# Attention and a four-expert layer on one core: the order of one product's terms, where weight splits stand, and which engine empties one bank

## The chip, the cores and the metric

The kernel runs on one core of a Trainium2 chip. The metric is the time of one execution on the device, in microseconds; the lower, the better. The kernel before was run three times: 935.79, 936.87 and 939.62 us, median 936.87 us.

## What is computed

Attention over 4 x 8 heads (sequence 576, head size 64, causal, with a decay that a running sum gives), then a layer of four experts over the 2304 tokens of 512 numbers that come out of it. All inputs and outputs are fp32. Cut to the expert layer, which is what the change touches:

```python
p = domain_probs / (domain_probs.sum(-1, keepdims=True) + 1e-09)
out = np.zeros((N, D), dtype=np.float32)           # N = 2304, D = 512
for e in range(E):                                 # E = 4
    h = np.maximum(x @ w1[e], 0.0)                 # w1[e]: 512 x 1024
    out += p[:, e:e + 1] * (h @ w2[e])             # w2[e]: 1024 x 512
```

## The kernel before

The program has two stretches. Up to about 386 us the attention runs, interleaved with expert 0, which is computed plainly; its order comes from a planner. From there on only experts 1 to 3 run, and their order is the order in which the code is written: each engine has its queue, and takes its instructions in that order.

Numbers are fp32, but PE multiplies a rounded form of them. So each operand is kept as a high part (a copy by ACT, `hi`, L457) and a low part (the operand less its high part, by DVE or POOL, `sub`, L444). A product is the sum of three terms: high by high, high by low, low by high.

An expert's 1024 hidden numbers are taken as two halves, so there are six halves for experts 1 to 3 (`HALVES`). For each half the tokens pass in three groups of 768 (`g` 0, 1, 2), which makes 18 items. An item has a first layer (x by w1) and a second layer (h by w2). Each is a 2 x 2 block product done with seven products instead of eight, numbered 1 to 7, at the price of sums of blocks made ahead. One product is 12 matmuls (128 x 128 by 384 columns): two output banks, and for each two slices of the sum and the three terms. `product` (L1262) writes them. The list of terms has the weights' low part third; with `late`, which only the first product of a second layer of group 0 uses (L1395), both banks get the first two terms first, and the low-weight terms follow for both.

The layers alternate: the first layer of item w + 1 stands ahead of the second layer of item w (loop at L1432). Banks: bA is pb0 and pb1, bB is pb2 and pb3, bC is pb4 and pb5, bM the two banks of mo.

- `first_layer` (L1284) runs products 1, 6, 5, 7, 2, 4, 3. Between them partial sums are passed on: by ACT from bank to bank (`pass_on`, L1273) or from a bank to SBUF (`keep`, L1297, L1300), by DVE with an addition (`plus`, L1305, L1307) and a gate (`gate` or `relu_op`, L1278), which is the relu and the token's probability. The results are four blocks, c11, c12, h21 and c22. From the second item on h21 is gated in its banks; for the first item DVE gates it from bA into SBUF.
- The blocks and their sums (s5, s6, s7, s3, DVE L1055) become the second layer's operands: high part by ACT, low part by DVE or POOL (hT, xg and hx). The tables `START`, `EARLY`, `REST` say after which product each is issued.
- `second_layer` (L1377) runs products 1, 6, 2, 5, 7, 3, 4. Product 1 goes to bC; ACT passes it on to bB, and product 6 is added to it in bC. DVE adds results to the accumulators (`update`, L1385).

The weights of a half are loaded whole, then `w_steps` (L1125) makes eight steps of them: the sums (POOL, L1055), and for each of the seven products a split of the weight block into high part (ACT) and low part. Parts 4 and 6 need sums that POOL makes after other parts are split. The steps wait in the list `side`; after each product one of them, none or two are issued (`after`, L1288 and L1389). For the second-layer weights of halves 1 to 5 the sums stand in the second layer of group 2 of the half before, and all seven splits in the first layer that follows it, in the order 5, 1, 6, 2, 7, 3, 4, with all low parts on DVE. For half 0 all stand in the first item's first layer.

Of the kernel before, what the change touches and what calls it, by code (L numbers as in the profile page):

```python
# [326 lines left out]
def body(ctx, tc, qk, qkv0, vp, s, dp, w1, w1s, w2, w2s, out):  # L327
# [21 lines left out]
    late = {}  # L349
# [775 lines left out]
    def w_steps(which, begin=False):  # L1125
# [19 lines left out]
        def split(o, e):  # L1145
            hi("ACT", part(o, 0), src[o])
            sub(e, part(o, 1), src[o], part(o, 0).bitcast(F32))
            if begin:
                pass
            elif o == 5 and neg:  # L1150
                add("POOL", src[6], src[5], b[1, 1], ALU.subtract)
            elif o == 5:
                add("POOL", src[6], b[1, 1], src[5], ALU.subtract)
            if o == 2 and not begin:
                add("POOL", src[4], src[4], src[6], ALU.add if neg else ALU.subtract)
# [4 lines left out]
            ((5, "DVE"), (1, "DVE"), (6, "DVE"), (2, "DVE"), (7, "DVE"), (3, "DVE"), (4, "DVE")))]  # L1160
# [101 lines left out]
    def product(o, x, ts, start, part=w1_part, late=False):  # L1262
        wv = [part(o, l).rearrange("p (k f) -> p k f", k=2) for l in range(2)]
        terms = list(enumerate(((0, 0), (0, 1), (1, 0))))
        for u, some in [(0, terms[:2]), (1, terms[:2]), (0, terms[2:]), (1, terms[2:])] if late else [(0, terms), (1, terms)]:
            for k, (n, (wl, xl_)) in [(k, x) for x in some for k in range(2)] if late else [(k, x) for k in range(2) for x in some]:
                nc.tensor.matmul(ts[u], wv[wl][:, k, 128 * u:128 * u + 128], x[xl_][:, k, :],  # L1267
                                 start=start and k == 0 and n == 0, stop=k == 1 and n == 2, skip_group_check=not start)

    def product2(o, ts, start, late=False):  # L1270
        product(o, [h_part(o, l) for l in range(2)], ts, start, w2_part, late)
# [12 lines left out]
    def first_layer(w_i, at, tmp):  # L1284
# [3 lines left out]
        def after(o):  # L1288
# [4 lines left out]
            for _ in range((0, 2)[o == 3] if side and w_i and o in (4, 3) else 1 if w_i else 2):  # L1293
                if side:
                    side.pop(0)()
# [41 lines left out]
        tmp["h21"] = bA if w_i else [(t := temp())[:, 0], t[:, 1]]  # L1337
        for u in range(2):
            relu_op("DVE", tmp["h21"][u], bA[u], gp[:, 1], ALU.mult)
# [37 lines left out]
    def second_layer(w_i, n, g, at):  # L1377
# [17 lines left out]
        product2(1, bC, True, g == 0)  # L1395
# [36 lines left out]
    for w_i, (n, g) in enumerate(work):  # L1432
# [20 lines left out]
        if g == 2 and more:  # L1453
            w2_next = w_steps(2)
            side.append(w2_next.pop(0))
# [35 lines left out]
```

## Time and profile before

| | before |
|---|---|
| time, median of 3 runs | 936.87 us (935.79 to 939.62) |
| the profiled execution: time, span | 936.36 us, 934.6 us |
| PE busy | 915.2 us, 98% |
| PE weight loads busy | 884.4 us, 95% |
| DVE busy | 691.4 us, 74% |
| ACT busy | 479.4 us, 51% |
| POOL busy | 486.2 us, 52% |
| chain that ended last | PE 81%, DVE 8%, ACT 4%, POOL 3%, issue 3% |

A profile is one execution. Its busy time counts, for each engine, the time in which an instruction ran; matmuls are pipelined, so a busy PE may still run below its pace. In the view of waits an engine's idle time is put down to the instruction that released it, the one that came last. In a timeline each row is one or several equal instructions in a queue, with the idle time ahead of the first and its releaser in brackets. DVE's "t<-pb" means that it reads a PSUM bank and writes to SBUF; "pb<-hT_r,w2h" is a matmul of the second layer with the high weights, "pb<-x,w1h" one of the first. Instructions that follow each other on DVE overlap by some hundredths of a microsecond in the rows.

### The profile page before, as it was taken

The page shows a single profiled execution, that of the slowest core. Times are in us where ns is not written, and L with a number is a line of the kernel's source. Part 1 is how long each engine was busy: PE and PEld are TensorE (multiplying, and loading weights), DVE is VectorE, ACT ScalarE, POOL GpSimd, SP SyncE. Part 2 cuts the span into 40 slices and gives each one's busy share as a digit, 9 for nine tenths or more (in the row PEclk, how much of TensorE's full clock was granted, in tenths as well). Part 3 has the DMA queues.
Part 4 walks back from the last instruction along what each step waited for, and adds up shares of the span by engine and source line. Part 5 has one row for each costly group of instructions (what it writes and reads, how often), then busy time and mean ns, then how long its engine had stood idle before and what let it go on. Part 6 is the DMA issues. An engine that isn't in the chain of part 4 may idle for free.

```text
span 934.6 us, 16455 instructions
## 1 busy us (share of the span) xinstructions
PE 915.2 (98%) x5590; PEld 884.4 (95%) x5590; DVE 691.4 (74%) x1575; ACT 479.4 (51%) x1092; POOL 486.2 (52%) x524
## 2 busy tenths in 40 slices
PE   9999999999999999999999999999999999999998
PEld 6789999899999999989998999899989998999898
DVE  7878888887851122597978787978796879687985
ACT  6898999998860111434335352535244433444342
POOL 4688887887734697211644363446144713571222
PEclk9999999999999999999999999999999999999999
DMA  6788888878516974596587547855686467755603
GB/s 169 185 253 245 221 232 227 236 209 250 165 55 222 372 266 162 168 341 235 185 298 236 177 172 266 268 188 170 226 297 211 158 220 263 251 161 169 236 30 118
DMA packets 131039, 198.85 MB, mean 213 GB/s; under 512 B 11448, under 2 KB 107772, under 8 KB 130956
## 3 DMA queue, kind: packets, MB, share of 16 engines
q1 hardware_dynamic: 130956, 197.81, 66.4%
q8 instruction: 44, 0.72, 0.3%
q14 instruction: 39, 0.32, 0.1%
HBM read 154.85 MB, written 29.05 MB: 197 GB/s over the span
## 4 chain that ended last, share of the span: by engine, by line
PE 81%; DVE 8%; ACT 4%; POOL 3%; issue 3%; DMA 0%; ACTq 0%; POOLq 0%; DVEq 0%
PE pb L1267 40%; PE mo L1267 8%; PE mo L950 7%; PE mo L936 6%; PE pv L835 4%; PE pb L936 4%; PE pb L950 3%; PE T L785 3%; PE S L739 2%; DVE t L1278 2%; PE S L736 1%; DVE t L1307 1%; ACT a L758 1%; PE X L785 1%; DVE w2l L444 1%
## 5 line engine op out<-in xcount | busy, mean ns | idle before, releaser
L1267 PE MATMUL pb<-x,w1h 128*128 128x384 f32 x1008 | 257.8, 336 | 1.9 <-DVE t L1278 1.9
L1267 PEld LDWEIGHTS pb<-x,w1h 128*128 128x128 f32 x1008 | 182.2, 189 | 3.8 <-DVE t L1278 2.2
L1267 PE MATMUL pb<-x,w1l 128*128 128x384 f32 x504 | 169.1, 335 | 0.0
L444 POOL TENSOR_TENSOR hT_r<-t,hT_r 128x768 fp32r<-128x768 f32 x17 | 32.1, 1888 | 254.1 <-PE pb L1267 218.9
L1275 ACT ACTIVATE pb<-pb 128x384 f32<-128x384 f32 x106 | 49.8, 475 | 157.4 <-DVE t L1307 90.6
L457 ACT ACTIVATE hT_r<-t 128x768 fp32r<-128x768 f32 x72 | 60.8, 845 | 104.0 <-PE pb L1267 97.4
L1267 PE MATMUL pb<-hT_r,w2h 128*128 128x384 f32 x432 | 107.4, 336 | 1.4 <-DVE t L1278 1.4
L1267 PEld LDWEIGHTS pb<-x,w1l 128*128 128x128 f32 x504 | 95.2, 189 | 0.0
L758 ACT ACTIVATE a<-a,mx 128x576 f32<-128x576 f32 (+4 forms) x136 | 81.0, 597 | 12.9 <-DVE mx L750 9.3
L1385 DVE TENSOR_TENSOR acc<-pb,acc 128x384 f32<-128x384 f32 x144 | 74.8, 551 | 15.8 <-PE pb L1267 12.9
L1267 PE MATMUL pb<-xg,w2h 128*128 128x384 f32 x288 | 74.0, 337 | 8.6 <-ACT pb L1275 8.6
L1267 PEld LDWEIGHTS pb<-hT_r,w2h 128*128 128x128 f32 x432 | 77.4, 188 | 3.3 <-DVE t L1278 3.3
L936 PE MATMUL mo<-xg,w1h 128*128 128x384 f32 (+1 forms) x304 | 78.3, 327 | 0.0
L452 POOL TENSOR_SCALAR a<-a,sm 128x576 f32<-128x576 f32 (+5 forms) x111 | 60.6, 552 | 28.4 <-DVE sm L766 15.0
L444 DVE TENSOR_TENSOR hT_r<-t,hT_r 128x768 fp32r<-128x768 f32 x55 | 57.6, 1049 | 21.1 <-ACT hT_r L457 19.9
L1267 PE MATMUL pb<-hT_r,w2l 128*128 128x384 f32 x216 | 69.3, 334 | 0.0
L1307 DVE TENSOR_TENSOR t<-pb,t 128x384 f32<-128x384 f32 x74 | 37.6, 549 | 34.6 <-ACT t L1300 23.4
L1267 PEld LDWEIGHTS pb<-xg,w2h 128*128 128x128 f32 x288 | 51.5, 188 | 10.9 <-ACT pb L1275 10.9
L1055 DVE TENSOR_TENSOR t<-t 128x768 f32<-128x768 f32 (+1 forms) x40 | 59.5, 1494 | 0.0
L950 PE MATMUL mo<-hT_r,w2h 128*128 128x256 f32 (+1 forms) x320 | 58.3, 314 | 0.0
L814 DVE TENSOR_TENSOR aTl<-T,aTh 128x256 fp32r<-128x256 f32 (+2 forms) x103 | 51.3, 508 | 4.9 <-ACT aTh L457 3.7
L750 DVE CUSTOM_DVE_ANT_0 a<-S,mask 128x448 f32<-128x448 f32 (+4 forms) x107 | 48.1, 456 | 7.5 <-PE S L736 5.8
(216 smaller groups left out, 2312.4 us busy)
## 6 DMA issues: line engine op xcount, KB each, us to landing
x<-xs_d SPq DMA_DIRECT2D x68, 768.0 KB
x<-x_d SPq DMA_DIRECT2D x55, 768.0 KB
xs_d<-x SPq DMA_DIRECT2D x12, 768.0 KB
KK<-AB_r SPq DMA_DIRECT2D x24, 288.0 KB
osb<-p_d SPq DMA_DIRECT2D x18, 384.0 KB
xg<-x_d SPq DMA_DIRECT2D x16, 384.0 KB
w1r<-in_w1s_dram SPq DMA_DIRECT2D x6, 1024.0 KB
w2r<-in_w2s_dram SPq DMA_DIRECT2D x6, 1024.0 KB
```

Of the source, the lines that this page charges most:

```text
L444: (nc.gpsimd if e == "POOL" else nc.vector).tensor_tensor(out=out, in0=in0, in1=in1, op=ALU.subtract)
L452: (nc.gpsimd if e == "POOL" else nc.vector).tensor_scalar(out, in_, scale, 1.0 if bias is None else bias, op0=ALU.mult, op1=ALU.mult if bi ...
L457: nc.scalar.activation(out, in_, AF.Copy)
L750: nc.vector.tensor_tensor_reduce(out=z[0:n, j0:j1], in0=tok["S", (c, pi)][0:n, 0:j1 - j0], in1=mask[0:n, 448 - a + j0:448 - a + j1], scale ...
L758: nc.scalar.activation(z[0:n, 0:bb], z[0:n, 0:bb], AF.Exp, bias=tok["mx", c][0:n, k:k + 1], scale=-1.0, accum_out=tok["sm", c][0:n])
L814: nc.vector.tensor_tensor(out=dst, in0=src, in1=h_.bitcast(F32), op=ALU.subtract)
L936: nc.tensor.matmul(t[:, 0:w], wl[q][:, dc, o:o + P], xgt[:, l, dc, 0:w], start=(u == 0), stop=(u == 3 * KD - 1))
L950: nc.tensor.matmul(t[:, 0:w], wl[fc // 2][:, fc % 2, 128 * dt:128 * dt + 128], ht[:, fc, 0:w], start=(u == 0), stop=(u == 3 * KF - 1))
L1055: (nc.gpsimd if e == "POOL" else nc.vector).tensor_tensor(out=out, in0=in0, in1=in1, op=op)
L1267: nc.tensor.matmul(ts[u], wv[wl][:, k, 128 * u:128 * u + 128], x[xl_][:, k, :], start=start and k == 0 and n == 0, stop=k == 1 and n == 2, ...
L1275: nc.scalar.activation(out[u], in_[u], AF.Copy)
L1385: nc.vector.tensor_tensor(out=d, in0=ts[u], in1=d, op=ALU.add)
```

## The change

Four things are changed. The first product of a second layer of group 0 uses the usual order of terms; `late` is gone. The second-layer weights are split in the order 1, 2, 5, 6, 7, 3, 4, with part 7's low part on POOL; the sum for part 4 is issued after part 6 instead of part 2. For halves 1 to 5 the sums and the splits 1, 2 and 5 stand in the second layer of group 2, and the splits 6, 7, 3 and 4 in the first layer behind it. For the first item h21 is copied out of bA by ACT and gated in SBUF by DVE.

```diff
--- before.py
+++ after.py
@@ -1151,13 +1151,13 @@
                 add("POOL", src[6], src[5], b[1, 1], ALU.subtract)
             elif o == 5:
                 add("POOL", src[6], b[1, 1], src[5], ALU.subtract)
-            if o == 2 and not begin:
+            if o == (6 if neg else 2) and not begin:
                 add("POOL", src[4], src[4], src[6], ALU.add if neg else ALU.subtract)
 
         return [sums] + [lambda o=o, e=e: split(o, e) for o, e in (
             tuple((o, "DVE") for o in PRODUCTS) if begin else
             ((5, "POOL"), (1, "POOL"), (2, "POOL"), (6, "POOL"), (4, "POOL"), (7, "DVE"), (3, "DVE")) if which == 1 else
-            ((5, "DVE"), (1, "DVE"), (6, "DVE"), (2, "DVE"), (7, "DVE"), (3, "DVE"), (4, "DVE")))]
+            ((1, "DVE"), (2, "DVE"), (5, "DVE"), (6, "DVE"), (7, "POOL"), (3, "DVE"), (4, "DVE")))]
 
     pmoe = ctx.enter_context(tc.tile_pool(name="psm", bufs=1, space=PSUM))
     pb = [pmoe.tile([P, 512], F32, name=f"pb{i}") for i in range(6)]
@@ -1259,16 +1259,16 @@
         n = (1, 2, 4, 5).index(o)
         return hT(l)[:, 2 * n:2 * n + 2, :]
 
-    def product(o, x, ts, start, part=w1_part, late=False):
+    def product(o, x, ts, start, part=w1_part):
         wv = [part(o, l).rearrange("p (k f) -> p k f", k=2) for l in range(2)]
         terms = list(enumerate(((0, 0), (0, 1), (1, 0))))
-        for u, some in [(0, terms[:2]), (1, terms[:2]), (0, terms[2:]), (1, terms[2:])] if late else [(0, terms), (1, terms)]:
-            for k, (n, (wl, xl_)) in [(k, x) for x in some for k in range(2)] if late else [(k, x) for k in range(2) for x in some]:
+        for u in range(2):
+            for k, (n, (wl, xl_)) in [(k, x) for k in range(2) for x in terms]:
                 nc.tensor.matmul(ts[u], wv[wl][:, k, 128 * u:128 * u + 128], x[xl_][:, k, :],
                                  start=start and k == 0 and n == 0, stop=k == 1 and n == 2, skip_group_check=not start)
 
-    def product2(o, ts, start, late=False):
-        product(o, [h_part(o, l) for l in range(2)], ts, start, w2_part, late)
+    def product2(o, ts, start):
+        product(o, [h_part(o, l) for l in range(2)], ts, start, w2_part)
 
     def pass_on(out, in_):
         for u in range(2):
@@ -1290,7 +1290,7 @@
                 xt[o] = load_operand(nxt[1], o)
             for f in at.get(o, ()):
                 f()
-            for _ in range((0, 2)[o == 3] if side and w_i and o in (4, 3) else 1 if w_i else 2):
+            for _ in range(2 if o == 3 or not w_i else 0 if o in (7, 2, 4) else 1):
                 if side:
                     side.pop(0)()
 
@@ -1334,9 +1334,14 @@
                 relu_op("DVE", tmp["c11"][:, u], bC[u], gp[:, 0], ALU.mult)
         after(2)
         product(4, x_of(4), bA, False)
-        tmp["h21"] = bA if w_i else [(t := temp())[:, 0], t[:, 1]]
-        for u in range(2):
-            relu_op("DVE", tmp["h21"][u], bA[u], gp[:, 1], ALU.mult)
+        if w_i:
+            tmp["h21"] = bA
+            for u in range(2):
+                relu_op("DVE", bA[u], bA[u], gp[:, 1], ALU.mult)
+        else:
+            keep("h21", bA)
+            gate("h21", 1)
+            tmp["h21"] = [tmp["h21"][:, u] for u in range(2)]
         after(4)
         product(3, x_of(3), bB, False)
         plus("c12", bB, 0)
@@ -1392,7 +1397,7 @@
             if side:
                 side.pop(0)()
 
-        product2(1, bC, True, g == 0)
+        product2(1, bC, True)
         pass_on(bB, bC)
         after(1)
         next_probs(w_i + 2)
@@ -1452,7 +1457,8 @@
             side.extend(w1_next)
         if g == 2 and more:
             w2_next = w_steps(2)
-            side.append(w2_next.pop(0))
+            side.extend(w2_next[:4])
+            del w2_next[:4]
         second_layer(w_i, n, g, plan(steps, EARLY if w_i + 2 < len(work) else ALL if w_i + 2 == len(work) else {}))
         while side:
             side.pop(0)()
```

Three places in the queues, ahead of and after the change.

ACT, first item, first layer, between the copies of c11 and c22 (w2h0 to w2h3 hold parts 1 and 2, 3 and 4, 5 and 6, and 7; L1300 are the copies of c12, then c22). Before:

```order
L457 ACTIVATE w2h2_86<-t2_4893 128x512
L1300 ACTIVATE t_4911<-pb0_3965 128x384
L1300 ACTIVATE t_4911<-pb1_3966 128x384
L457 ACTIVATE w2h0_84<-w2r_4191 128x512
L457 ACTIVATE w2h2_86<-t2_4893 128x512
L457 ACTIVATE w2h0_84<-w2r_4191 128x512
L457 ACTIVATE w2h3_87<-w2r_4191 128x512
L1300 ACTIVATE t_4951<-pb0_3965 128x384
L1300 ACTIVATE t_4951<-pb1_3966 128x384
```

After:

```order
L457 ACTIVATE w2h0_84<-w2r_4191 128x512
L1300 ACTIVATE t_4910<-pb0_3965 128x384
L1300 ACTIVATE t_4910<-pb1_3966 128x384
L457 ACTIVATE w2h0_84<-w2r_4191 128x512
L457 ACTIVATE w2h2_86<-t2_4893 128x512 x2
L457 ACTIVATE w2h3_87<-w2r_4191 128x512
L1300 ACTIVATE t_4951<-pb0_3965 128x384
L1300 ACTIVATE t_4951<-pb1_3966 128x384
```

Parts 1 and 2 now come first, and the split of part 6, which reads POOL's sum t2, follows that of part 5 directly.

POOL, from the sums in the second layer of group 2 to the end of the first layer behind it (t2 becomes part 6, w2r the sums of parts 7 and 4; hT1, xg and hx are low parts of operands). Before:

```order
L1055 TENSOR_TENSOR t2_5672<-w2r_5269 128x512
L1055 TENSOR_TENSOR w2r_5269<-w2r_5269 128x512
L444 TENSOR_TENSOR hT1_r_600<-t_5690,hT0_r_593 128x768
L1055 TENSOR_TENSOR t2_5672<-t2_5672,w2r_5269 128x512
L444 TENSOR_TENSOR xg_92<-t_5709,xg_92 128x768
L444 TENSOR_TENSOR hx_4874<-t_5562,hx_4874 128x768
L1055 TENSOR_TENSOR w2r_5269<-w2r_5269,t2_5672 128x512
```

After:

```order
L1055 TENSOR_TENSOR t2_5673<-w2r_5270 128x512
L1055 TENSOR_TENSOR w2r_5270<-w2r_5270 128x512
L1055 TENSOR_TENSOR t2_5673<-t2_5673,w2r_5270 128x512
L444 TENSOR_TENSOR hT1_r_600<-t_5691,hT0_r_593 128x768
L1055 TENSOR_TENSOR w2r_5270<-w2r_5270,t2_5673 128x512
L444 TENSOR_TENSOR xg_92<-t_5712,xg_92 128x768
L444 TENSOR_TENSOR w2l3_91<-w2r_5270,w2h3_87 128x512
L444 TENSOR_TENSOR hx_4874<-t_5563,hx_4874 128x768
```

The sum of part 6 has moved ahead of operand 5, the sum of part 4 ahead of xg, and part 7's low part stands between xg and hx.

DVE, second layer of group 2, from the sum s5 to the update from mo (w2l0 holds the low parts of parts 1 and 2). Before:

```order
L1055 TENSOR_TENSOR t_5690<-t_5598,pb0_3965 128x384
L1055 TENSOR_TENSOR t_5690<-t_5598,pb1_3966 128x384
L1385 TENSOR_TENSOR acc0_4_3941<-pb2_3967,acc0_4_3941 128x384
L1385 TENSOR_TENSOR acc1_4_3947<-pb3_3968,acc1_4_3947 128x384
L444 TENSOR_TENSOR hT1_r_600<-t_5562,hT0_r_593 128x768
L1055 TENSOR_TENSOR t_5709<-t_5618,pb0_3965 128x384
L1055 TENSOR_TENSOR t_5709<-t_5618,pb1_3966 128x384
L1385 TENSOR_TENSOR acc2_5_3954<-mo_0_102,acc2_5_3954 128x384
```

After:

```order
L1055 TENSOR_TENSOR t_5691<-t_5599,pb0_3965 128x384
L1055 TENSOR_TENSOR t_5691<-t_5599,pb1_3966 128x384
L444 TENSOR_TENSOR w2l0_88<-w2r_5270,w2h0_84 128x512
L1390 TENSOR_TENSOR acc0_4_3941<-pb2_3967,acc0_4_3941 128x384
L1390 TENSOR_TENSOR acc1_4_3947<-pb3_3968,acc1_4_3947 128x384
L444 TENSOR_TENSOR hT1_r_600<-t_5563,hT0_r_593 128x768
L1055 TENSOR_TENSOR t_5712<-t_5619,pb0_3965 128x384
L1055 TENSOR_TENSOR t_5712<-t_5619,pb1_3966 128x384
L444 TENSOR_TENSOR w2l0_88<-w2r_5270,w2h0_84 128x512
L1390 TENSOR_TENSOR acc2_5_3954<-mo_0_102,acc2_5_3954 128x384
L1390 TENSOR_TENSOR acc3_5_3960<-mo_1_103,acc3_5_3960 128x384
```

Two low parts stand ahead of the update from mo; that of part 5 follows behind the next sum, and these three have left the first layer behind it.

## Rows read from the trace of the kernel before

**Rows 1.** The page, part 1: busy us (share of the span), instructions.
```profile
PE 915.2 (98%) x5590; PEld 884.4 (95%) x5590; DVE 691.4 (74%) x1575; ACT 479.4 (51%) x1092; POOL 486.2 (52%) x524
```

**Rows 2.** Waits of PE from 350 us: waiter, released by, us, times, longest.
```profile
PE pb L1267 <- ACT pb L1275: 8.6, 6, 1.8
PE pb L1267 <- DVE t L1278: 3.3, 6, 1.9
```

**Rows 3.** Timeline of PE: start us, us, operation, count [idle before <-releaser].
```profile
403.10 0.87 PE L1267 MATMUL pb<-x,w1h 128*128 128x384 f32 x2 [1.92 <-DVE t L1278]
...
422.43 0.62 PE L1267 MATMUL pb<-xg,w2h 128*128 128x384 f32 x2 [0.51 <-ACT pb L1275]
...
460.12 0.62 PE L1267 MATMUL mo<-hx,w2h 128*128 128x384 f32 x2
...
489.38 0.51 PE L1267 MATMUL mo<-hx,w2h 128*128 128x384 f32 x2
...
493.54 0.51 PE L1267 MATMUL pb<-x,w1h 128*128 128x384 f32 x2
...
508.76 1.66 PE L1267 MATMUL pb<-hT_r,w2h 128*128 128x384 f32 x8 [0.27 <-DVE t L1278]
...
512.69 0.62 PE L1267 MATMUL pb<-xg,w2h 128*128 128x384 f32 x2 [1.58 <-ACT pb L1275]
...
599.10 1.14 PE L1267 MATMUL pb<-hT_r,w2h 128*128 128x384 f32 x5 [0.28 <-DVE t L1278]
```

**Rows 4.** Timeline of DVE at the boundary before the second half.
```profile
498.33 1.97 DVE L444 TENSOR_TENSOR w2l<-t,w2h 128x512 fp32r<-128x512 f32 x1 [0.29 <-ACT w2h L457]
...
500.22 0.94 DVE L1055 TENSOR_TENSOR t<-t 128x768 f32<-128x768 f32 x1
...
503.01 2.11 DVE L444 TENSOR_TENSOR w2l<-t,w2h 128x512 fp32r<-128x512 f32 x1
...
506.09 1.54 DVE L1278 SCALAR_TENSOR_TENSOR t<-t,osb 128x768 f32<-128x768 f32 x1
...
507.56 0.68 DVE L444 TENSOR_TENSOR w2l<-w2r,w2h 128x512 fp32r<-128x512 f32 x1
...
508.16 1.01 DVE L1278 SCALAR_TENSOR_TENSOR t<-pb,osb 128x384 f32<-128x384 f32 x2
...
511.06 1.01 DVE L1307 TENSOR_TENSOR t<-pb,t 128x384 f32<-128x384 f32 x2
```

**Rows 5.** Timeline of POOL: first item, then the same boundary.
```profile
390.55 1.29 POOL L1055 TENSOR_TENSOR t<-t,w2r 128x512 f32<-128x512 f32 x1 [9.18 <-DVE w2l L444]
...
497.86 1.88 POOL L444 TENSOR_TENSOR hT_r<-t,hT_r 128x768 fp32r<-128x768 f32 x1 [19.59 <-PE pb L1267]
...
502.28 2.30 POOL L444 TENSOR_TENSOR xg<-t,xg 128x768 fp32r<-128x768 f32 x1
...
508.38 1.28 POOL L1055 TENSOR_TENSOR w2r<-w2r,t 128x512 f32<-128x512 f32 x1 [1.56 <-DVE w2l L444]
```

**Rows 6.** Timeline of ACT: first item, then the same boundary.
```profile
391.88 0.63 ACT L457 ACTIVATE w2h<-t 128x512 fp32r<-128x512 f32 x1
...
501.19 0.85 ACT L457 ACTIVATE hx<-t 128x768 fp32r<-128x768 f32 x1 [0.89 <-DVE t L1055]
...
502.88 0.85 ACT L1300 ACTIVATE t<-pb 128x384 f32<-128x384 f32 x2
...
512.16 0.86 ACT L1275 ACTIVATE pb<-pb 128x384 f32<-128x384 f32 x2 [1.84 <-DVE t L1307]
```

**Rows 7.** Timeline of DVE: first item, two second layers of the first half.
```profile
395.50 1.02 DVE L1307 TENSOR_TENSOR t<-pb,t 128x384 f32<-128x384 f32 x2 [1.06 <-ACT t L1300]
...
420.80 1.01 DVE L1307 TENSOR_TENSOR t<-pb,t 128x384 f32<-128x384 f32 x2
...
459.52 1.01 DVE L1385 TENSOR_TENSOR acc<-mo,acc 128x384 f32<-128x384 f32 x2
...
488.10 1.01 DVE L1385 TENSOR_TENSOR acc<-mo,acc 128x384 f32<-128x384 f32 x2
```

## The prediction

> **What bounds the kernel now.** I read the page's busy table first: PE is busy 98% of the span [rows 1], so only PE's own idle time, and the slow restart behind it, can be won back. The view of waits names that time [rows 2]: 8.6 us in six waits on ACT's copies out of pb, and 3.3 us in six waits on DVE's line L1278. Then I took PE's timeline [rows 3]. Between product 3 of a second layer (489.38) and the next first layer (493.54) lie two products, so one product of 12 matmuls takes 2.08 us, and a half (six layers of seven products) would take 42 x 2.08 = 87.4 us. From one boundary between halves to the next (508.76 to 599.10) it takes 90.3 us: **3.0 us are lost in each of the last five halves**. Where: seven products after 493.54 the second layer could start its first product at 508.10 and its second at 510.18; that second one starts at 512.69, 2.5 us late, and its first matmuls run some 0.1 us behind pace. That is 2.6 us, all at this boundary; the other 0.4 us of a half stand elsewhere.
>
> The releaser in that row is ACT, but ACT has waited itself: its copies start at 512.16 [rows 6], just after DVE has read the same bank in c12's addition, started at 511.06 [rows 4]. DVE is the late one. In the first layer ahead of the boundary it does five low-part subtractions of second-layer weights, and they are long while POOL runs: 1.97 and 2.11 us, where 0.68 us is the short price [rows 4]. Two rows side by side show why: POOL's xg subtraction runs from 502.28 to 504.58, and DVE's w2l that starts at 503.01 ends 0.54 us after it; a POOL instruction of the same shape took 1.88 us at 497.86 and this one 2.30 [rows 4, 5]. Such instructions, with both inputs in SBUF, take turns. DVE's pairs with one input in PSUM keep to 1.0 us [rows 4].
>
> So the usual order of terms in the first product wins nothing alone: PE waits for c12's addition, not for its own matmuls. What counts is how much earlier DVE reaches that addition.
>
> **Part 1, splits moved into the second layer ahead (five times).** DVE's queue there gets the splits of parts 1 and 2 ahead of the update that empties mo, and that of part 5 behind it. POOL has nothing to do in that stretch, so each takes the short 0.68 us, some 0.6 net, since an instruction starts a little before the one ahead has ended (506.09 + 1.54 is 507.63, the next starts at 507.56) [rows 4]. Today that update starts at 488.10 [rows 7]; two splits push it to 489.3. What a late update costs is seen in the layer where first-layer weights are split: the update starts at 459.52 and product 3 at 460.12, 0.60 later [rows 3, 7]. So product 3 starts at 489.9 in place of 489.38 [rows 3]: 0.5 us and 0.1 for the restart, **0.6 us lost, a new wait**. Behind it stand all later products, and DVE's third split, for which DVE has idle time there. The ACT halves of these splits, 0.63 us each [rows 6], fall where ACT waits for products.
>
> **Part 2, the first layer behind it.** All times there are 0.6 us later. DVE has two w2l left (parts 6 and 3); part 7 is POOL's. Step by step: POOL's operand 5 starts at 498.5 (497.86 [rows 5] and 0.6), takes 1.88 and ends at 500.4; DVE's split 6 waits for it and ends at 501.0. POOL's sum of part 4 stood at 508.38, held by a DVE w2l [rows 5]; now nothing holds it, so it takes its turn, 1.29 us at the price of its shape [rows 5], to 502.3. The next DVE instruction, the sum s3 that ran at 500.22 for 0.94 [rows 4], waits for that and ends at 503.2. ACT makes hx from it (0.85 [rows 6]), then the high half of part 3 (0.63), and is free for c22's copies at 504.5, where they started at 502.88 [rows 6]. PE's product 4 needs the first half of that bank, free at 505.0; by pace it would start at 504.5. **Another new wait of about 0.5 us, 0.6 with the restart.** DVE adds c22 at 505.5 (1.0 us), gates it after one wait for POOL's part 7, to 507.7, empties two banks in 1.9 us, and adds c12 at 509.5, against 511.06 today, although everything lies 0.6 later. PE follows 1.6 us behind the start of that addition (511.06 to 512.69 [rows 3, 4]): 511.1. PE, two waits late, asks for it at 510.18 + 1.2 = 511.4. So no wait is left there. At the boundary 2.6 us go and 1.2 us come: **1.4 us won, 7.0 us in five halves**.
>
> **Part 3, the first item.** Here PE waits 1.92 us at 403.10 for h21, which DVE reads out of bA late [rows 3]. After the change ACT copies it out: with c22 added from 396.5 (below) and gated by 398.5, operand 4 (0.85) and two splits (0.63 each) keep ACT till 400.5, and the copies (0.85) till 401.3, so this wait all but goes. But DVE's chain is what is late: it runs nearly without a gap from c22's addition at 395.50 to c12's at 420.80, and PE's second product of the second layer, at 422.43, follows 1.63 us behind [rows 3, 7]. The chain keeps its length, as h21's gate costs DVE about the same from SBUF (0.94 like s3, against a pair of 1.0 [rows 4]). And its head gets later. Before, part 5 was split first, so POOL made part 6 at 390.55 and ACT split it at 391.88, in time [rows 5, 6]. Now part 5 comes third: ACT splits it from 391.8, DVE ends at 393.1, POOL runs from 393.2 to 394.5 (1.29 us), and ACT's splits of parts 6 and 7 stand in its queue ahead of c22's copies (0.63 each). DVE, which could add c22 at 395.50, does so at 396.5, **1.0 us later**. Everything behind shifts, so 422.43 becomes 423.4: 1.0 us lost. PE's wait does not go, it moves: to product 6 of the next first layer, where the bank's copy stands in ACT's queue behind an operand that waits for DVE (about 1.8 us), then to products 7, 4 and 3 of that layer and to the boundary.
>
> **Sum.** 7.0 won, 1.0 lost: 6.0 us from the profiled execution's 936.36, which lies 0.5 us under the median 936.87 of the runs: 930.4 to 930.9, and I take **930.5 us**. About 0.5% (4.7 us) is what a measurement of this kernel can tell from no change, so faster means under 932.2.
>
> **Rivals.**
> - *All these waits go.* If DVE gets its turn ahead of POOL's freed sum, and the two splits fit into DVE's slack in the second layer, five boundaries give 5 x 2.6 = 13 us: 923.4. For: both new waits are short of nothing by half a microsecond only. Against: the update at 459.52 and product 3 at 460.12 show that wait in a like layer [rows 3, 7]. Chance 0.15.
> - *POOL takes back what it is given.* Each POOL instruction with two SBUF inputs takes a turn of 1.29 us where the DVE split it replaces took 0.68 [rows 4, 5]. If s3 and c22's gate together lose 1.6 us more than I allow, c12's addition is back at 511.06 and the boundary stays as it is: 936.4 and the first item's 1.0 are 937.4, and with the second layer's 0.6 in each half 940.4. For: the rows of 1.97 and 2.11 us are of this kind. Against: three subtractions have left that layer. Chance 0.15. The Trainium skill, SBUF — State Buffer, section Who interferes with whom, says that POOL's only port pair is DVE's second one, and that whichever starts first holds it for its whole instruction; the trace agrees, with 2.11 us in place of 0.68 beside POOL [rows 4]. By that rule a split given to POOL frees DVE only while DVE works from PSUM, and the time would be this rival's.
> - *Slower.* The splits put into the second layer cost the long price there. Two of 2.0 us ahead of mo's update push it to 492.1 and product 3 to 492.7, 3.4 us late with the restart; with the first layer's 0.6 that is 4.0 us for 2.6 gained, in five halves 7 us, and the first item's 1.0: 944.4. It decides if POOL is busy there; the change breaks even when that update starts near 490.5. For: the w2l rows with the long price. Against: POOL's next instruction waits for part 5's split, which is behind the update. Chance 0.07.
> - *The change does not do what it says*, because a queue puts the moved work where it was: the lists of queues show it moved, so 0.03, at 936.4.
>
> **How the numbers follow.** My forecast has 0.60, with its own range of 927 to 933 (each new wait between 0.2 and 1.1 us, the first item between 0 and 2 us lost); 0.51 of it lies under 932.2. Faster: 0.51 + 0.15 = 0.66. Slower by over 0.5% (over 941.5): the slower rival and 0.01 of POOL's, 0.08. Same: the other 0.26. The range 922.5 to 939.0 leaves out the slower rival, the late end of POOL's and a third of the first rival's, together under 0.2.
>
> **What would show it.** Right: the wait at the second layer's second product falls from 1.6 us to nothing in five halves; a wait of 0.3 to 0.6 us on DVE's mo update appears in the third second layer of a half, and one on ACT's copy of c22 at product 4 behind it; in the first item the wait at 403.10 is gone, one of 1.5 to 2 us stands one product later, and DVE's c12 addition comes near 421.8. Wrong: c12's addition still 2 us behind PE's product 3, or a w2l of 2 us in the second layer, or a first item that ends earlier than 422.43.

## The result and the profile after

The changed kernel takes **928.46 us** (median of four runs, 927.86 to 928.90) against 937.38 us for the kernel before (median of four runs, 935.79 to 939.62). The ratio is 0.9903, with a 95% interval of 0.9881 to 0.9925: 8.9 us faster. The forecast was 930.5 us, with a range of 922.5 to 939.0.

The profiled execution of the changed kernel took 928.90 us, with a span of 927.1 us. Its busy table, the line that answers to [rows 1]:

```profile
PE 914.6 (99%) x5590; PEld 884.6 (95%) x5590; DVE 676.2 (73%) x1568; ACT 480.0 (52%) x1094; POOL 498.5 (54%) x530
```

PE's busy time is as before (914.6 against 915.2 us); the span has shrunk around it. DVE is 15 us less busy and POOL 12 us more. PE's waits from 350 us on, the view that answers to [rows 2] (waiter, released by, us in total, times, longest):

```profile
PE pb L1267 <- ACT pb L1275: 2.1, 2, 1.6
PE mo L1267 <- DVE acc L1390: 1.2, 5, 0.2
PE pb L1267 <- DVE t L1307: 1.0, 1, 1.0
PE pb L1267 <- DVE t L1278: 0.8, 1, 0.8
PE pb L1267 <- ACT t L1300: 0.4, 1, 0.4
```

Of the 8.6 us in six waits on ACT's copies 2.1 us in two are left, both in the first item; 1.2 us in five waits on DVE's mo update are new. PE's timeline (start us, us, operation, count, idle before with its releaser), first item and first half, against [rows 3]:

```profile
387.61 0.52 PE L1267 MATMUL pb<-x,w1h 128*128 128x384 f32 x2
...
406.04 0.61 PE L1267 MATMUL pb<-x,w1h 128*128 128x384 f32 x2 [1.60 <-ACT pb L1275]
...
418.40 0.62 PE L1267 MATMUL pb<-x,w1h 128*128 128x384 f32 x2 [0.97 <-DVE t L1307]
...
424.42 0.62 PE L1267 MATMUL pb<-xg,w2h 128*128 128x384 f32 x2 [0.54 <-ACT pb L1275]
...
491.81 0.62 PE L1267 MATMUL mo<-hx,w2h 128*128 128x384 f32 x2 [0.24 <-DVE acc L1390]
...
513.01 0.33 PE L1267 MATMUL pb<-xg,w2h 128*128 128x384 f32 x1
...
601.49 0.33 PE L1267 MATMUL pb<-xg,w2h 128*128 128x384 f32 x1
```

The same timeline, weight loads, at product 4 of the boundary's first layer:

```profile
506.64 0.30 PEld L1267 LDWEIGHTS pb<-x,w1h 128*128 128x128 f32 x2 [0.31 <-ACT t L1300]
```

The start of a second layer's second product is a good clock for a half, because the old wait stood there. From 513.01 to 601.49 are 88.48 us, where the kernel before takes 90.3; the five halves take 442.51 us in all (424.42 to 866.93), before 451.83 (422.43 to 874.26). So 9.3 us are won in the halves. The first item loses some: from its first matmul to its second layer's second product it takes 36.81 us (387.61 to 424.42), before 35.97 (386.45 to 422.43). Together that is 8.5 us, and 0.1 us more behind the last boundary: 8.6 us from the first matmul of this stretch to the last. The attention ahead of it, where no instruction has changed, took 1.16 us longer in this execution (first matmul at 387.61 against 386.45), so the two profiled executions lie only 7.5 us apart; in the runs below that start lies anywhere between 386.17 and 387.80.

DVE, POOL and ACT, the rows that answer to [rows 4 to 7]. DVE, c22's addition in the first item, then the boundary:

```profile
397.66 1.02 DVE L1307 TENSOR_TENSOR t<-pb,t 128x384 f32<-128x384 f32 x2
...
487.27 0.69 DVE L444 TENSOR_TENSOR w2l<-w2r,w2h 128x512 fp32r<-128x512 f32 x1
...
490.60 0.69 DVE L444 TENSOR_TENSOR w2l<-w2r,w2h 128x512 fp32r<-128x512 f32 x1
...
491.21 1.02 DVE L1390 TENSOR_TENSOR acc<-mo,acc 128x384 f32<-128x384 f32 x2
...
493.00 0.69 DVE L444 TENSOR_TENSOR w2l<-t,w2h 128x512 fp32r<-128x512 f32 x1
...
502.76 2.05 DVE L1055 TENSOR_TENSOR t<-t 128x768 f32<-128x768 f32 x1
...
506.24 0.82 DVE L444 TENSOR_TENSOR w2l<-w2r,w2h 128x512 fp32r<-128x512 f32 x1 [1.43 <-ACT w2h L457]
507.00 1.02 DVE L1307 TENSOR_TENSOR t<-pb,t 128x384 f32<-128x384 f32 x2
508.05 0.99 DVE L1278 SCALAR_TENSOR_TENSOR t<-t,osb 128x768 f32<-128x768 f32 x1
...
511.13 1.02 DVE L1307 TENSOR_TENSOR t<-pb,t 128x384 f32<-128x384 f32 x2 [0.22 <-PE pb L1267]
```

POOL:

```profile
502.25 1.74 POOL L1055 TENSOR_TENSOR w2r<-w2r,t 128x512 f32<-128x512 f32 x1
...
506.46 1.76 POOL L444 TENSOR_TENSOR w2l<-w2r,w2h 128x512 fp32r<-128x512 f32 x1
```

ACT, in the first item (the copies of c22) and at the boundary:

```profile
396.77 0.86 ACT L1300 ACTIVATE t<-pb 128x384 f32<-128x384 f32 x2
...
504.84 0.85 ACT L457 ACTIVATE hx<-t 128x768 fp32r<-128x768 f32 x1 [1.99 <-DVE t L1055]
...
506.11 0.85 ACT L1300 ACTIVATE t<-pb 128x384 f32<-128x384 f32 x2
...
512.24 0.47 ACT L1275 ACTIVATE pb<-pb 128x384 f32<-128x384 f32 x1 [4.76 <-DVE t L1307]
```

Three things are to be seen. The three splits in the second layer (487.27, 490.60, 493.00) take the short 0.69 us each. c12's addition at 511.13 waits 0.22 us for PE: DVE now arrives ahead of PE's product, so ACT copies from 512.24, and PE does not wait at 513.01. And the price stands earlier: product 3 of the second layer at 491.81 follows the mo update at 491.21 by 0.60 us.

### The profile page after: what moved, and what is told of

Same layout as the page of the kernel before. It is cut to its first block, busy times and chain, and to the rows that moved or that the text cites. A ratio compares the mean times of both kernels' runs of the same rounds, so it can differ in the third digit from the quotient of the medians.

```text
span 927.1 us, 16473 instructions
## 1 busy us (share of the span) xinstructions
PE 914.6 (99%) x5590; PEld 884.6 (95%) x5590; DVE 676.2 (73%) x1568; ACT 480.0 (52%) x1094; POOL 498.5 (54%) x530
## 4 chain that ended last, share of the span: by engine, by line
PE 84%; DVE 8%; ACT 4%; issue 2%; POOL 1%; DMA 0%; SPq 0%; ACTq 0%; POOLq 0%
PE pb L1267 43%; PE mo L1267 7%; PE mo L950 7%; PE mo L936 6%; PE pv L835 4%; PE pb L936 4%; PE pb L950 3%; PE T L785 3%; PE S L739 3%; PE S L736 1%; DVE acc L1390 1%; DVE hT_r L444 1%; DVE t L1055 1%; PE X L785 1%; ACT a L758 1%
## 5 line engine op out<-in xcount | busy, mean ns | idle before, releaser
L1267 PE MATMUL pb<-hT_r,w2h 128*128 128x384 f32 x432 | 109.7, 334 | 0.8 <-DVE t L1278 0.8
L1267 PE MATMUL pb<-hT_r,w2l 128*128 128x384 f32 x216 | 72.2, 334 | 0.0
L1055 DVE TENSOR_TENSOR t<-t 128x768 f32<-128x768 f32 (+1 forms) x40 | 65.0, 1632 | 0.0
L936 PEld LDWEIGHTS mo<-xg,w1h 128*128 128x128 f32 x304 | 52.1, 190 | 1.4 <-issue 0.7
```

The lines of the kernel that those rows point to most:

```text
L936: nc.tensor.matmul(t[:, 0:w], wl[q][:, dc, o:o + P], xgt[:, l, dc, 0:w], start=(u == 0), stop=(u == 3 * KD - 1))
L1055: (nc.gpsimd if e == "POOL" else nc.vector).tensor_tensor(out=out, in0=in0, in1=in1, op=op)
```

## The experiments

All are edits of the kernel before or of the changed kernel; each was run beside the kernel before, whose median in these sets lies between 937.8 and 938.2 us. "Half" is the distance between the second products of two second layers, as above. Because the start of this stretch lies up to 1.6 us apart between the profiled executions, effects of about 1 us are read from the traces, with the medians beside them.

**1. The order of terms alone, in the kernel before.**

```diff
-        product2(1, bC, True, g == 0)
+        product2(1, bC, True)
```

> The kernel before with one edit: the first product of a second layer uses the usual order of terms. Theory (PE waits there for DVE's addition of c12, not for its own matmuls): nothing moves. PE's wait ahead of the second product of the second layer keeps 1.5 to 1.9 us idle in five halves, the time between boundaries stays at 90.3 us (within 0.2), the time at 937 us. Rival (the late order holds the bank, so ACT copies late): that wait falls under 0.3 us, a half takes 88.6 us, the time falls by 8 us to about 929.

Measured: 937.87 us, ratio 1.0002 (0.9992 to 1.0012); a half takes 90.3 us as before. The order alone wins nothing, because PE waits for c12's addition, not for its own matmuls.

One half of this execution took 91.91 us. Its boundary wait is followed by slow matmuls; PE's row there, then the granted clock in three stretches behind the wait (stretch, PE busy, instructions, clock in parts of full speed, DMA share, GB/s):

```profile
783.74 0.62 PE L1267 MATMUL pb<-xg,w2h 128*128 128x384 f32 x2 [1.85 <-ACT pb L1275]
```

```profile
783.80:785.50 1.70, 1.70 (x9) 0.92 0.48 159
785.70:788.70 3.00, 3.00 (x11) 0.51 0.77 262
789.00:791.00 2.00, 2.00 (x14) 1.00 0.52 201
```

A clock of 0.51 is the lower of the two levels, 1.2 in place of 2.4 GHz. The eleven matmuls from 785.60 on each took some 0.15 us longer, 1.6 us in all. The kernel before had the same idle time of 1.85 us at 783.92, and no such stretch behind it:

```profile
404.00:405.00 1.00, 1.00 (x4) 0.50 1.08 378
783.90:786.00 2.10, 2.08 (x12) 1.00 0.54 166
```

It had one behind its wait of 1.92 us at 403.10 [rows 3]: there the clock is 0.50.

**2. h21 by ACT alone, in the kernel before.**

```diff
-        tmp["h21"] = bA if w_i else [(t := temp())[:, 0], t[:, 1]]
-        for u in range(2):
-            relu_op("DVE", tmp["h21"][u], bA[u], gp[:, 1], ALU.mult)
+        if w_i:
+            tmp["h21"] = bA
+            for u in range(2):
+                relu_op("DVE", bA[u], bA[u], gp[:, 1], ALU.mult)
+        else:
+            keep("h21", bA)
+            gate("h21", 1)
+            tmp["h21"] = [tmp["h21"][:, u] for u in range(2)]
```

> The kernel before with one edit: the first item's h21 is copied out of its banks by ACT and gated in SBUF. Theory (DVE's chain from c22's addition to c12's sets the first item, PE's wait only moves): the wait of 1.92 us is gone, a wait of 0.7 to 1.0 us stands at product 6 of the next first layer, others follow, and from the first item's first matmul to the second product of its second layer it takes 36.0 us as before (within 0.3); the time does not change measurably. Rival (that wait is worth its 1.9 us and the slow stretch behind it): 32.5 to 34 us, and the time falls by 2 to 3.5 us.

Measured: 937.94 us, 1.0005 (0.9994 to 1.0016); the first item takes 35.82 us, before 35.97; in run 1, whose first item differs from that only in the order of terms, it takes 35.81. PE's wait at 403.10 is gone, others stand behind it, the first at 403.98 with 0.63 us idle, a little under the 0.7 to 1.0 expected. The wait moves and is not won.

**3. The changed kernel with the late order of terms.**

```diff
...
-        product2(1, bC, True)
+        product2(1, bC, True, g == 0)
```

> The changed kernel with the late order of terms put back in. Theory (with DVE in time the order of the terms is what ends last at the boundary): the first bank is complete after 10 of 12 matmuls in place of 6, 0.7 us later, so a wait of PE on ACT's copy of 0.3 to 0.5 us comes back in five halves, a half takes 88.9 us against 88.5, the time is 930 to 931.5. Rival (order means nothing): 88.5 us a half, 928.5. In the first item no difference in either, since DVE's addition is still late there.

Measured: 930.19 us, 0.9921 (0.9904 to 0.9937); a half takes 88.97 us, 0.49 more than the changed kernel. PE's timeline at the boundary:

```profile
510.97 0.86 PE L1267 MATMUL pb<-hT_r,w2l 128*128 128x384 f32 x4
...
512.04 0.61 PE L1267 MATMUL pb<-xg,w2h 128*128 128x384 f32 x2 [0.21 <-ACT pb L1275]
```

With the late order the first bank is finished only by the low-weight matmuls of 510.97, ACT copies it later, and a small wait is back at 512.04. The order of terms is worth nothing where DVE is late (run 1) and 0.5 us a half, 2.4 us in all by the traces (1.7 us by the medians), where DVE is in time.

**4. The changed kernel with the first item's old order of splits.** The table and the place of part 4's sum are those of before for the first item only, all low parts on DVE.

```diff
...
+            ((5, "DVE"), (1, "DVE"), (6, "DVE"), (2, "DVE"), (7, "DVE"), (3, "DVE"), (4, "DVE")) if first else
             ((1, "DVE"), (2, "DVE"), (5, "DVE"), (6, "DVE"), (7, "POOL"), (3, "DVE"), (4, "DVE")))]
...
```

> The changed kernel with the old order of weight splits, all on DVE, in the first item alone. Theory (the new order delays part 6, which stands in ACT's queue ahead of c22's copies, by 1.0 us): c22's addition comes 9.0 us behind the first item's first matmul in place of 10.0, and from that matmul to the second product of its second layer it takes 35.9 to 36.1 us in place of 36.8; the time falls by 0.8 us to 927.7. Rival (ACT's copy of h21, standing in ACT's queue, is what costs): 36.8 us stay, and the time stays at 928.5.

Measured: 927.63 us, 0.9890 (0.9875 to 0.9904). The first item takes 35.82 us against 36.81; the halves stay at 88.5. DVE's addition of c22 comes 9.05 us behind the first matmul (386.57) again, 10.05 in the changed kernel (the line numbers are one higher in this file):

```profile
395.62 1.02 DVE L1308 TENSOR_TENSOR t<-pb,t 128x384 f32<-128x384 f32 x2 [1.06 <-ACT t L1301]
```

So the first item's 1.0 us is the price of the new table, and the copies of h21 are not part of it. The edit takes back three things at once, the order, part 7 on POOL and the place of part 4's sum. Part 7 on POOL is not what costs: with it alone back on DVE (run 5) the first item takes 37.27 us. The place of part 4's sum was not run alone.

**5. The changed kernel with part 7's low part on DVE.**

```diff
-((1, "DVE"), (2, "DVE"), (5, "DVE"), (6, "DVE"), (7, "POOL"), (3, "DVE"), (4, "DVE"))
+((1, "DVE"), (2, "DVE"), (5, "DVE"), (6, "DVE"), (7, "DVE"), (3, "DVE"), (4, "DVE"))
```

> The changed kernel with part 7's low part on DVE instead of POOL. Theory (DVE and POOL take turns where both inputs are in SBUF, so one more DVE split in the crowded first layer costs a turn of POOL as well): DVE adds c12 1 to 2 us behind PE's product 3, PE waits 0.7 to 2 us at the boundary and ahead of product 3, a half takes 89.5 to 90.5 us in place of 88.5, the time is 933.5 to 938.5. Rival (it is one short instruction of 0.68 us, and DVE has 0.5 us of slack there): a half takes 88.5 to 88.8 us, the time is at most 930.

Measured: 937.35 us, 0.9991 (0.9973 to 1.0010), a half 90.25 us, the first item 37.27: nearly all of the gain is gone. DVE's and POOL's timelines show what one split more costs:

```profile
505.23 4.60 DVE L444 TENSOR_TENSOR w2l<-w2r,w2h 128x512 fp32r<-128x512 f32 x2
...
509.75 1.01 DVE L1307 TENSOR_TENSOR t<-pb,t 128x384 f32<-128x384 f32 x2
```

```profile
504.45 2.56 POOL L444 TENSOR_TENSOR xg<-t,xg 128x768 fp32r<-128x768 f32 x1
...
506.96 2.31 POOL L444 TENSOR_TENSOR hx<-t,hx 128x768 fp32r<-128x768 f32 x1
```

The splits of parts 7 and 3 take 4.60 us together, beside POOL's xg and hx, and c22's addition starts at 509.75; PE waits 1.30 us for it, ahead of product 3 at 510.81. In the changed kernel one split took 0.82 us there (506.24). One split more, of a kind that takes 0.68 us where POOL is idle, cost 1.8 us a half here.

**6. The changed kernel with no spreading:** all seven splits in the first layer again, in the new order, with part 7 on POOL.

```diff
-            side.extend(w2_next[:4])
-            del w2_next[:4]
+            side.append(w2_next.pop(0))
...
-            for _ in range(2 if o == 3 or not w_i else 0 if o in (7, 2, 4) else 1):
+            for _ in range((0, 2)[o == 3] if side and w_i and o in (4, 3) else 1 if w_i else 2):
```

> The changed kernel with all seven splits back in the first layer (new order, part 7 on POOL, usual order of terms), only the sums in the second layer. Theory (spreading is what wins): the wait on DVE's mo update in the third second layer is gone (0.5 us a half), but c12's addition is 1.5 us or more late again; a half takes 89.2 to 90.3 us, the time is 932 to 937. Rival (moving part 7 to POOL and the order win, spreading adds only the mo wait): a half takes 88.0 us, the time is 926.

Measured: 940.85 us, 1.0046 (1.0022 to 1.0069), a half 91.04 us: the boundary's gain is lost, as expected, but the loss goes further than the 932 to 937 us expected: the time is above that of the kernel before. PE's timeline at the boundary:

```profile
511.12 0.62 PE L1267 MATMUL pb<-hT_r,w2h 128*128 128x384 f32 x2 [1.04 <-DVE t L1278]
...
514.01 0.61 PE L1267 MATMUL pb<-xg,w2h 128*128 128x384 f32 x2 [0.51 <-ACT pb L1275]
```

The four splits that DVE does ahead of it:

```profile
498.89 1.97 DVE L444 TENSOR_TENSOR w2l<-w2r,w2h 128x512 fp32r<-128x512 f32 x1 [0.29 <-ACT w2h L457]
...
503.31 0.68 DVE L444 TENSOR_TENSOR w2l<-w2r,w2h 128x512 fp32r<-128x512 f32 x1
504.82 1.90 DVE L444 TENSOR_TENSOR w2l<-t,w2h 128x512 fp32r<-128x512 f32 x1 [0.83 <-ACT w2h L457]
...
508.82 1.78 DVE L444 TENSOR_TENSOR w2l<-t,w2h 128x512 fp32r<-128x512 f32 x1
```

Three run beside POOL's work, at the long price; the one at 503.31 finds POOL idle. The last, part 6, stands late because it reads a sum that POOL makes only after part 5's low part (504.82), and in this order part 5 comes third; that this makes the loss larger was read from the rows, not tested. The waits on DVE's gate (1.04 at 511.12) and on ACT's copy (0.51 at 514.01) stand in place of the old single one, with one of 0.54 us at 505.21 and a smaller one behind it in the layer ahead. So the new order and POOL's share together lose 0.7 us a half without the spreading, and the spreading wins 2.6 us a half (91.04 to 88.48).

**7. The changed kernel with no split behind product 2 of that second layer,** so that only one split stands ahead of the mo update.

```diff
-            if side:
+            if side and not (g == 2 and o == 2):
                 side.pop(0)()
```

> The changed kernel with one step moved: in the third second layer no split is issued after product 2, so parts 2 and 5 are split after products 5 and 7. Theory (the new wait of 0.5 us ahead of product 3 is the price of two splits ahead of DVE's mo update, and DVE has idle time behind it): the wait of 0.24 us idle, 0.4 us behind pace with its restart of 0.1, goes, a half takes 87.9 to 88.0 us in place of 88.5, the time falls by 2.5 us to about 926. Rival (DVE's work is only pushed on and is paid at the boundary): 88.5 us a half, 928.5.

Measured: 925.72 us, 0.9872 (0.9849 to 0.9894), a half 87.95 us. DVE's update from mo and PE's product 3:

```profile
490.82 1.02 DVE L1390 TENSOR_TENSOR acc<-mo,acc 128x384 f32<-128x384 f32 x2
```

```profile
491.62 0.51 PE L1267 MATMUL mo<-hx,w2h 128*128 128x384 f32 x2
```

Product 3 starts without a wait. The first of the two new waits costs 0.53 us a half, by taking it away.

**8. The changed kernel with operand 3 issued behind product 7,** in all first layers but the last, so that ACT copies c22 out of its banks before it makes that operand's high part. This takes away the second new wait alone.

```diff
-REST = {1: "6 5", 6: "s3 7", 5: "3"}
+REST = {1: "6 5", 6: "s3 7", 7: "3"}
...
-            at = plan(steps, REST if w_i else FIRST)
+            at = plan(steps, (REST if w_i + 2 < len(work) else {**REST, 7: "", 5: "3"}) if w_i else FIRST)
```

> The changed kernel with one table entry changed: in all first layers but the last, operand 3 is issued behind product 7 and not behind product 5, so ACT copies c22 out of its banks before it makes that operand's high part. It tests the second new wait by itself, forecast at 0.6 us and read at 0.26 us. Theory of the reading: 0.26 us a half goes, half period 88.2, 1.3 us in five halves, 927.2 us. By the forecast's size it would be 0.6 us a half, period 87.9, 925.5 us. Rival: POOL's low part of that operand moves behind as well and takes a turn with DVE's gate of c22 (1.27 us alone, 2.44 us beside POOL); c12's addition, which had only 0.22 us to spare, comes up to 1 us late, a wait of up to 1 us returns at the boundary, half period about 89.2, 932 us.

Measured: 926.33 us, 0.9882 (0.9866 to 0.9899), a half 88.2 us (88.18 to 88.32), 0.28 less than the changed kernel; the wait of 506.64 has no counterpart. The wait is worth 0.26 to 0.28 us, not 0.6. The rival did not come: DVE's gate of c22 started 0.15 us ahead of POOL's operand and took 1.00 us. The 1.27 us that the expectation calls its price alone is that of a gate which starts inside a POOL instruction (889.51 in the trace of after, POOL's hx from 888.11 for 1.86 us); alone it takes 0.96 us (512.18).

```profile
506.92 1.00 DVE L1278 SCALAR_TENSOR_TENSOR t<-t,osb 128x768 f32<-128x768 f32 x1
```

```profile
507.07 2.56 POOL L444 TENSOR_TENSOR hx<-t,hx 128x768 fp32r<-128x768 f32 x1
```

**9. All of it: a faster version.** Operand 3 behind product 7; the sum s7 (an SBUF addition of DVE) behind the mo update in every second layer; the first item with its old order of splits, its tables loosened, and the low parts of parts 3 and 4 on POOL.

```diff
-EARLY = {1: "1", 6: "s5", 2: "2 s7", 5: "s6", 4: "4"}
-REST = {1: "6 5", 6: "s3 7", 5: "3"}
+EARLY = {1: "1", 6: "s5", 2: "2", 5: "s7 s6", 4: "4"}
+REST = {1: "6 5", 6: "s3 7", 7: "3"}
...
-FIRST = {1: "2 5 s6", 6: "6", 5: "s3 7", 7: "3"}
+FIRST = {1: "2 5 s6", 6: "6", 5: "s3", 7: "7", 2: "3"}
...
+            ((5, "DVE"), (1, "DVE"), (6, "DVE"), (2, "DVE"), (7, "DVE"), (3, "POOL"), (4, "POOL")) if first else
...
```

> The changed kernel with four moves: in every second layer the sum s7 stands behind DVE's update from mo; operand 3 is issued after product 7 of a first layer, so that ACT copies c22 ahead of it; in the first item the old order of splits with the low parts of 3 and 4 on POOL; in the second item operand 7 behind product 7 and operand 3 behind product 2. Theory (each wait found is one late instruction in a queue): the waits ahead of product 3 (0.25 and 0.5 us a half) and ahead of product 4 (0.26) go, a half takes 87.4 to 87.7 us, the first item 33.5 to 35 us in place of 36.8; the time is 920 to 923. Rival (the engines are full, so each wait taken away comes back elsewhere): a half takes 88.3 us or more, the time is 926 or more.

Measured: 920.28 us, 0.9815 (0.9797 to 0.9834). A half takes 87.4 us, the first item 32.90, less than the 33.5 to 35 expected. Of these moves only operand 3 was run alone (run 8); of the 3.9 us in the first item run 4 gives 1.0 to its table, and the rest is not divided. But the stretch behind the last boundary takes 57.43 us where the changed kernel takes 56.29: PE waits at the last second layer but one. PE, then DVE and POOL ahead of it (the line numbers are one higher in this file and the next):

```profile
887.13 0.62 PE L1268 MATMUL pb<-xg,w2h 128*128 128x384 f32 x2 [1.00 <-ACT pb L1276]
```

```profile
879.42 2.44 DVE L1279 SCALAR_TENSOR_TENSOR t<-t,osb 128x768 f32<-128x768 f32 x1
```

```profile
879.20 1.85 POOL L444 TENSOR_TENSOR hx<-t,hx 128x768 fp32r<-128x768 f32 x1 [1.14 <-issue]
```

The last first layer has no splits, and POOL's operand 3, now later, gets its turn 0.22 us ahead of DVE's gate of c22: the gate takes 2.44 us, and all that DVE does behind it is late.

**10. The same, with operand 3 back behind product 5 in that last first layer.**

```diff
-            at = plan(steps, REST if w_i else FIRST)
+            at = plan(steps, (REST if w_i + 2 < len(work) else {**REST, 7: "", 5: "3"}) if w_i else FIRST)
```

> The fastest version so far, with one thing taken back: in the last first layer, which has no weight splits, the third operand is issued behind product 5 again and not behind product 7. Theory (the new wait of 1.17 us near the end came from c22's gate, which there took a turn with POOL's low part of that operand): the wait goes, the rest stays, 919.0 to 919.4 us against 920.28. Rival (the gate is late for another reason, the operand's place does not matter): the time stays at 920.3 and a wait of about 1 us stands at the second product of the last second layer but one.

Measured: **918.35 us** (918.28 to 919.58), 0.9801 (0.9786 to 0.9816); it is the fastest, ahead of both kernels. The gate (878.94) takes 1.27 us, the wait is gone, and the stretch behind the last boundary takes 56.29 us again. That is 1.14 us. The medians lie 1.9 us apart, which goes below the 919.0 expected; in the profiled executions the rest lies ahead of this stretch, which starts at 386.36 in place of 386.82:

```profile
878.94 1.27 DVE L1279 SCALAR_TENSOR_TENSOR t<-t,osb 128x768 f32<-128x768 f32 x1
```

PE's waits that are left from 386 us on:

```profile
PE pb L1268 <- ACT t L1301: 0.9, 1, 0.9
PE pb L1268 <- ACT pb L1276: 0.2, 1, 0.2
```

Both stand in the first item. A half takes 87.39 us; PE's own pace over the half was worked out as 87.4 ahead of the change. What is left in this stretch is mostly in the first item: its 15 products of 2.08 us would take 31.2 us, and it takes 32.89.

## Why the prediction was right, and where its sizes were off

**What bounds it: right.** DVE's late addition of c12 set the boundary. Run 1 shows that the order of terms alone does nothing, and the trace of after that the wait goes once DVE is in time (511.13, idle 0.22 for PE). There the order has changed too; run 3 parts the two. With DVE in time and the late order kept, 0.49 us a half come back, so some 2.1 of the 2.6 us are DVE's lateness, and the order is worth the rest only behind it. What it is worth then the prediction did not say.

**Part 1: right.** Forecast 0.6 us lost on the mo update; the trace has product 3 at 491.81, 0.41 us behind PE's pace (from start to start of the two matmuls, less the 0.17 us of one at pace), and the first matmul behind the wait another 0.11: 0.52. Taking it away gave 0.53 (run 7). The splits took the short price, as said; the rival that ends slower rested on 2.0 us each and fell with that.

**Part 2: the mechanism right, the size wrong.** This is the term that was mis-sized: "another new wait of about 0.5 us, 0.6 with the restart", at product 4. It is there, released by ACT's copy of c22, but PE is only 0.16 us behind its pace at 506.64, and 0.11 more for the restart: 0.26 us, and run 8 won 0.28 by taking it away. The chain ahead of it ran in the order described, POOL's freed sum (502.25) ahead of DVE's s3 (502.76), hx on ACT (504.84), the copies at 506.11. The forecast's times are to be read 2.0 us later here, 1.16 from the attention and 0.84 from the first item: it put the copies at 504.5, so 506.5, and they came 0.4 us sooner. POOL's operand 5, DVE's split 6, POOL's sum and DVE's s3 each ended 0.05 to 0.14 us sooner behind the one ahead than was allowed; an instruction that waits for its turn shows as started already inside the other (502.76 lies within 502.25 + 1.74). Why these steps are shorter than an end-to-start sum was not tested. Five halves by 0.34 us are 1.7 of the 2.3 us that the halves gave beyond the forecast; Part 1's 0.08 gives 0.4; one half of before that took 90.63 us, not 90.3, gives 0.3; and the first half of the changed kernel, with 88.59 us, takes 0.1 back.

**The boundary: right.** 2.6 us go at each. c12's addition was put at 509.5, so 511.5 here; it starts at 511.13 and no wait is left. DVE was free before that and waited 0.22 us for PE: the turn behind POOL's part 7 that the forecast allowed for c22's gate came to almost nothing (508.05, 0.99 us).

**POOL as the other side.** The rival in which POOL takes back what it is given did not come. Its condition was that s3 and c22's gate lose 1.6 us more than was allowed; s3 ended at 504.81, where 505.2 was allowed by these times, and the gate took 0.99 us. But the margin is narrow: with all splits in the first layer the time is 940.85 (run 6), beside that rival's 937.4 to 940.4, and with part 7 back on DVE it is 937.35 (run 5). The Trainium skill, SBUF — State Buffer, section Who interferes with whom, has a DVE instruction with two SBUF inputs contend with a GpSimd instruction that reads SBUF. The rows agree: 4.60 us for two splits beside POOL in run 5, 0.69 us each with POOL idle in the trace of after. In the changed kernel POOL's part 7 (506.46) runs while DVE adds c22 from PSUM, which keeps its 1.02 us (507.00); run 5 shows what the same part costs on DVE.

**Part 3, the first item: right.** c22's addition stands 10.05 us behind the first matmul (397.66), directly behind ACT's copies of c22 (396.77), before 9.05: the 1.0 us that was forecast. The loss at the end is 0.84 us by the trace, 0.8 us by the times of run 4. It is 1.0 us against run 1, whose first item takes 35.81 us with the old table and without the slow stretch that the kernel before had behind 403.10. The waits moved as said: the one that stood at 403.10 is gone, 406.04 has 1.60 us (forecast about 1.8), and 410.84, 418.40, 421.53 and 424.42 have the rest; product 4 of that layer has none, which the forecast had.

**The sum.** 6.0 us were forecast, 8.6 us came by the traces of this stretch and 8.9 us by the medians. The 2.6 us beyond the forecast are 2.3 in the halves, 0.16 in the first item and 0.1 behind the last boundary. The later place of part 4's sum, one piece of the change, was not run alone. 928.46 lies inside the forecast's own range of 927 to 933. The rival in which all these waits go (923.4) did not come; runs 7 and 8 each take one of them away, and run 10, which also mends the first item, ends below it.

## What to carry to other kernels

Before an edit at the place where an engine waits, follow the releaser back until it is an engine that did not wait itself; here an order of matmuls was worth nothing until DVE had been moved, and 2.4 us after that. Where two engines take turns, count an instruction at the price of the place where it will stand, not at its short price: a split took 0.7 us beside an idle POOL, and one more of them beside a busy one cost 1.8 us. And when one wait of a layer goes, the next smallest slack decides: each of the two new waits here was won afterwards by moving one instruction behind another that PE needs sooner (runs 7 and 8).

## What was not expected of the hardware

PE's clock did not answer alike to like waits. Behind an idle time of 1.85 us it fell to 0.51 in run 1 and stayed at 1.00 in the trace of before, at the same place; in run 2 it fell there too (1.86 us ahead of 783.89, clock 0.50 from 785.0 to 788.0, the half 91.86 us). In the first item it is the other way round: behind 1.92 us it fell to 0.50 in the trace of before (403.10) and stayed at 1.00 in run 1 (403.06). Behind the 1.60 us at 406.04 of the changed kernel it stayed at 1.00:

```profile
406.10:408.00 1.90, 1.90 (x11) 1.00 0.78 278
```

The stretch of run 1 cost 1.6 us. The runs of the kernel before spread over 3.8 us (935.79 to 939.62), those of the changed kernel, where no wait of more than 1.6 us is left in this stretch, over 1.0 us. But run 6 has no longer wait than 1.6 us either, and one of its seven runs took 946.97 us beside 940.30 to 941.17 for the others. That the slow stretches make the wider spread was not tested, and what decides whether one comes is open.
